# Attention and two MoE layers in one program: VectorE's small scratch tiles start one float32 column further in, and five one-column steps with two tensors take a column as scalar instead

## The chip, the cores and the metric

One Trainium2 chip, one core. The metric is the device time of one execution in microseconds (us); lower is better. A TensorE (PE), a VectorE (DVE), a ScalarE (ACT) and a GpSimd engine (POOL) work side by side, each through its own instructions in their order; SyncE (SP) issues the transfers.

## The reference

Chunked attention with 8 memory keys, then two feed-forward layers on the 3072 tokens that come out of it. What is computed, cut down:

```python
# q, k, v: (4, 8, 768, 64) float32; weights 512x2048 and 2048x512 (float64 words in memory)
for c in range(nc):                       # chunks of 32 queries, 16 left, 8 right
    k_full = concatenate([mem_k, k_ctx]); v_full = concatenate([mem_v, v_ctx])
    scores = scale * q_c @ k_full.T
    scores = scores - max(scores)
    a = exp(scores); a = a / (sum(a) + 1e-9)
    out[chunk] = a @ v_full
h = x @ w_in                              # first layer
g = maximum(h, 0) + alpha * minimum(h, 0)
x = g @ w_out
h = x @ w_in2                             # second layer
g = h * sigmoid(1.702 * h)
out = g @ w_out2
```

## The kernel before, in words

The tokens are cut into 12 blocks of 256. Products on TensorE are made from float16 parts, so every float32 operand is scaled by a power of two and split into a high part (ACT, L129, "hi") and a low part (VectorE, L132, "lo": the value times its scale less the high part).

The weights lie in memory as float64 words. `w_dec_b` (L200, L201, L207) makes float32 of them on VectorE with bit operations on 128x1024, with the sign for some by POOL (L205); `w_split_a` and `w_split_b` split them on ACT (L211) and POOL (L216). Their scales are worked out by `w_scale` (L179 to L189) on one or two columns.

Attention goes block by block: `att_scale` takes the maxima of q, k and v (three columns of `ar`) through `pow2_scale` (L108 to L112), L340 forms the scale of the exponential, then q, k and v are split (L129, L132). The scores of a block are made in two halves `i` by 16 matmuls each (L482, L483), copied from PSUM by ACT (`att_ext`, L497 and L499), and `att_smax` (L509, L510), `att_exp` (L514), `att_sum` (L519 to L523) and `att_a16` (L528, L529) follow. The block's output is scaled like q, through the same `pow2_scale` with one column (`att_xall`, L413, `att_xs`), and split to `xt`, on which layer 1 works.

Layer 1 is `h` on TensorE (L580), `t` on ACT (L615), `gf` on VectorE (L618), a split of `gf` to `g` (ACT L129 or L641 and L642; VectorE L132 or POOL L643) and the second matmul (L660). Layer 2 takes its operands in seven sums and differences (L591, L674), with `y_scale` (L715, L718) and `l2_scale` (L724 to `l2t`) ahead of each pair of blocks.

A table written by hand gives each function of attention, weights and evacuation a time; the order of the instructions on each engine is then set by the framework's scheduler from its own estimate of each instruction's duration (the `TileContext` is made with the timeline scheduling on). So an instruction of another kind can move others.

POOL works on 128x512 and 128x1024 tiles between VectorE's steps: L205, L216, L241, L510, L523, L529 and L643.

Of the kernel before, what the change touches and what calls it, by code (L numbers as in the profile page):

```python
# [8 lines left out]
F32 = mybir.dt.float32  # L9
# [4 lines left out]
ALU = mybir.AluOpType  # L14
# [22 lines left out]
def kernel(  # L37
# [14 lines left out]
    nc = tc.nc  # L52
    B, H, S, D = q.shape
# [16 lines left out]
    scale = 1.0 / float(D) ** 0.5  # L70

    HF = NP // 2
    const = ctx.enter_context(tc.tile_pool(name="const", bufs=1))
    sm_p = ctx.enter_context(tc.tile_pool(name="sm", bufs=2))
# [20 lines left out]
    wcs, winv, wful = ([const.tile([128, NP], F32, name=f"{n}{m}") for m in range(3)] for n in ("wcs", "winv", "wful"))  # L95
    for x in (wcs, winv, wful):
        x[2:] = [x[2][:, 0:HF], x[2][:, HF:NP]]
    l2t = const.tile([128, 2, HF], F32, name="l2t")
    l2t = [l2t[:, i] for i in range(2)]
    eye = const.tile([128, 128], F32, name="eye")  # L100
    make_identity(nc, eye)
    blk = [const.tile([128, 16], F32, name=f"blk{b}") for b in range(NB)]

    def pow2_scale(m, s, inv, lo):
        n = m.shape[1]
        t = sm_p.tile([128, 4], F32, tag="pt", name="pt", bufs=1)[:, 0:n]
        f = sm_p.tile([128, 4], F32, tag="pf", name="pf", bufs=1)[:, 0:n]
        nc.vector.tensor_scalar(out=t, in0=m, scalar1=lo, scalar2=None, op0=ALU.max)  # L108
        nc.vector.tensor_scalar(out=f.bitcast(U32), in0=t.bitcast(U32), scalar1=EXPM, scalar2=None, op0=ALU.bitwise_and)
        nc.vector.tensor_scalar(out=inv, in0=f, scalar1=2.0 ** -13, scalar2=None, op0=ALU.mult)  # L110
        nc.vector.reciprocal(out=t, in_=inv)
        nc.vector.tensor_scalar(out=s.bitcast(U32), in0=t.bitcast(U32), scalar1=EXPM, scalar2=None, op0=ALU.bitwise_and)  # L112
# [12 lines left out]
    def absmax(o, i):  # L125
        nc.vector.tensor_reduce(out=o, in_=i, axis=AX.X, op=ALU.max, apply_absolute_value=True)  # L126
# [46 lines left out]
    def w_scale(m, a, z):  # L173
        r = wmax[1][:, a:z] if m == 1 else wtmp.pop(("r", m, a))
        n = z - a
        ws = sm_p.tile([128, 6, 4], F32, tag="ws", name="ws")
        t, f, u, v, c, d = (ws[:, i, 0:n] for i in range(6))
        cs, inv, ful = wcs[m][:, a:z], winv[m][:, a:z], wful[m][:, a:z]
        nc.vector.tensor_scalar(out=t, in0=r, scalar1=2.0 ** -14, scalar2=1.0 / (1.375 if m > 1 else 1.625), op0=ALU.max, op1=ALU.mult)  # L179
        nc.vector.tensor_scalar(out=c, in0=r, scalar1=2.0 ** -14, scalar2=2.0 ** -112, op0=ALU.max, op1=ALU.mult)  # L180
        nc.vector.tensor_scalar(out=f.bitcast(U32), in0=t.bitcast(U32), scalar1=EXPM, scalar2=None, op0=ALU.bitwise_and)
        nc.vector.tensor_scalar(out=d.bitcast(U32), in0=c.bitcast(U32), scalar1=3, scalar2=EXPM, op0=ALU.logical_shift_left, op1=ALU.bitwise_and)
        nc.vector.reciprocal(out=v, in_=f)
        nc.vector.tensor_scalar(out=u, in0=f, scalar1=2.0 ** -113, scalar2=None, op0=ALU.mult)
        nc.vector.tensor_scalar(out=v, in0=v, scalar1=2.0 ** -111, scalar2=None, op0=ALU.mult)
        nc.vector.tensor_scalar(out=ful, in0=d, scalar1=2.0 ** -13, scalar2=None, op0=ALU.mult)
        nc.vector.tensor_scalar(out=cs.bitcast(U32), in0=v.bitcast(U32), scalar1=EXPM, scalar2=None, op0=ALU.bitwise_and)
        nc.vector.tensor_scalar(out=u.bitcast(U32), in0=u.bitcast(U32), scalar1=3, scalar2=None, op0=ALU.logical_shift_left)
        nc.vector.tensor_scalar(out=inv, in0=u, scalar1=2.0 ** 7, scalar2=None, op0=ALU.mult)  # L189
# [88 lines left out]
    att = {}  # L278

    def geo(nb):  # L280
        b, j = divmod(nb, S // TB)
        return b, j * TB

    def eng(nb):
        return nc.vector if nb == 0 else nc.gpsimd

    def bs(nb, i):
        return blk[nb][:, i:i + 1]
# [44 lines left out]
    def att_all(nb, a, z):  # L333
        att["r", nb] = all_max(blk[nb][:, a:z])

    def att_scale(nb, a, z):
        w = blk[nb]
        pow2_scale(att.pop(("r", nb)), w[:, 3 + a:3 + z], w[:, 6 + a:6 + z], 2.0 ** -30)
        if a == 0:
            nc.vector.scalar_tensor_tensor(out=w[:, 9:10], in0=w[:, 6:7], scalar=scale, in1=w[:, 7:8], op0=ALU.mult, op1=ALU.mult)  # L340

    def att_hi(nb, i):
        if i == 0:
# [66 lines left out]
        absmax(bs(nb, i), att["xp", nb, i].rearrange("p j t -> p (j t)"))  # L410

    def att_xall(nb):
        nc.vector.tensor_tensor(out=bs(nb, 2), in0=bs(nb, 0), in1=bs(nb, 1), op=ALU.max)  # L413
        att_all(nb, 2, 3)

    def att_xs(nb):
        w = blk[nb]
        pow2_scale(att.pop(("r", nb)), w[:, 9:10], w[:, 6:7], 2.0 ** -16)
        nc.vector.tensor_scalar(out=w[:, 8:9], in0=w[:, 6:7], scalar1=1.0 / AS, scalar2=None, op0=ALU.mult)
# [65 lines left out]
    def att_ext(nb, i):  # L485
        sc = at_p.tile([128, 9, SL], F32, tag="sc", name="sc", bufs=2)
        b, t0 = geo(nb)
        t1 = t0 + 128 * i
        sv = sc.rearrange("p (a b) s -> p a b s", a=3)
        pv = sps[:, :, 0:3 * TW].rearrange("p a (b t) -> p a b t", b=3)  # L490
        mo = 0 if i == 0 else BAND
        bo = NM if i == 0 else 0
        parts = [(sv, pv)]
        if nb in F32B:
            parts = [(sc[:, 0:6].rearrange("p (b a) s -> p a b s", a=2), pv[:, 0:2]), (sc[:, 6:8], pv[:, 2, 0:2])]
        for d, x in parts:
            nc.scalar.copy(d[..., WIN:SL], x[..., mo:mo + NM])  # L497
            for c in range(4):
                nc.scalar.copy(d[32 * c:32 * c + 32, ..., 0:WIN], x[32 * c:32 * c + 32, ..., bo + CH * c:bo + CH * c + WIN])  # L499
        if t1 == 0:  # L500
            eng(nb).memset(sc[0:32, 0:H, 0:LEFT], NEG)
        if t1 + 128 == S:
            nc.gpsimd.memset(sc[96:128, 0:H, WIN - RIGHT:WIN], NEG)
        att["s", nb, i] = sc[:, 0:H]

    def att_smax(nb, i):
        sc = att["s", nb, i]
        mx = at_p.tile([128, H, 1], F32, tag="mx", name="mx", bufs=2)
        nc.vector.tensor_reduce(out=mx, in_=sc, axis=AX.X, op=ALU.max)  # L509
        eng(nb).tensor_tensor(out=sc, in0=sc, in1=mx.to_broadcast([128, H, SL]), op=ALU.subtract)  # L510

# [3 lines left out]

    def att_sum(nb, i):
        sc = att["s", nb, i]
        sm = at_p.tile([128, H, 1], F32, tag="smm", name="smm", bufs=2)
        nc.vector.tensor_reduce(out=sm, in_=sc, axis=AX.X, op=ALU.add)  # L519
        nc.vector.tensor_scalar(out=sm, in0=sm, scalar1=1e-9, scalar2=1.0 / AS, op0=ALU.add, op1=ALU.mult)  # L520
        rs = at_p.tile([128, H, 1], F32, tag="rs", name="rs", bufs=2)
        nc.vector.reciprocal(out=rs, in_=sm)
        eng(nb).tensor_tensor(out=sc, in0=sc, in1=rs.to_broadcast([128, H, SL]), op=ALU.mult)  # L523

# [187 lines left out]

    def y_scale(sb):
        w, v = blk[2 * sb], blk[2 * sb + 1]
        nc.vector.tensor_tensor(out=w[:, 11:12], in0=w[:, 11:12], in1=v[:, 11:12], op=ALU.max)  # L715
        pow2_scale(w[:, 11:12], w[:, 12:13], w[:, 14:15], 2.0 ** -100)
        for x in (w, v):
            nc.vector.tensor_tensor(out=x[:, 10:11], in0=w[:, 12:13], in1=x[:, 8:9], op=ALU.mult)  # L718

    def l2_scale(sb):  # L720
        t = sm_p.tile([128, 1], F32, tag="l2", name="l2", bufs=1)
# [91 lines left out]
        nc.sync.dma_start(out=al, in_=alpha.rearrange("(f p) -> p f", p=128))  # L813

    def alpha_prep():
        t = sm_p.tile([128, 4], F32, tag="pt", name="pt", bufs=1)
        nc.vector.tensor_scalar(out=oma, in0=al, scalar1=-1.0, scalar2=1.0, op0=ALU.mult, op1=ALU.add)
        absmax(t[:, 0:1], al)
        amx = all_max(t[:, 0:1])
        nc.vector.tensor_scalar(out=t[:, 1:2], in0=amx, scalar1=1.0, scalar2=None, op0=ALU.max)  # L820
        nc.vector.tensor_scalar(out=t[:, 2:3].bitcast(U32), in0=t[:, 1:2].bitcast(U32), scalar1=EXPM, scalar2=None, op0=ALU.bitwise_and)
        nc.vector.tensor_scalar(out=kl[:, 1:2], in0=t[:, 2:3], scalar1=2.0 ** 23, scalar2=None, op0=ALU.mult)
        nc.vector.reciprocal(out=t[:, 3:4], in_=kl[:, 1:2])
        nc.vector.tensor_scalar(out=kl[:, 0:1].bitcast(U32), in0=t[:, 3:4].bitcast(U32), scalar1=EXPM, scalar2=None, op0=ALU.bitwise_and)
# [94 lines left out]
    for g in range(NP):  # L919
        m, p = 2 + g % 2, g // 2  # L920
        t = 24 * (g + 3) - 8 + EX3
# [12 lines left out]
    for b in range(NB):  # L934
        t = 3 * ((NP * (b + 1) if b >= NA else HF * (NA + b + 1)) + L0) + 2 - 3
# [7 lines left out]
    for sb in range(NB // 2):  # L943
        t = Q0 + 48 * sb
# [3 lines left out]
        t = 48 * sb + 80 if sb else 101.5  # L948
# [3 lines left out]
        if sb == NB // 2 - 1:  # L952
            t = Q0 + 20
# [11 lines left out]
    at_p = l1.enter_context(tc.tile_pool(name="at", bufs=1))  # L965
# [62 lines left out]
    for q in range(STEPS // 2 + LQ):  # L1028
        t = Q0 + 6 * q
# [13 lines left out]
        else:  # L1043
            while done < min(2 * STEPS // 2, 2 * q + 2 - LQ):
                u = units[done]
# [5 lines left out]
        if xs:  # L1051
            sb, p = divmod(q, NP)
# [33 lines left out]
```

## Time and profile before

| | |
|---|---|
| median of 3 runs | 1194.43 us (1193.17 to 1195.58) |
| span of the profiled execution | 1188.6 us |
| time of the profiled execution itself | not given apart from its span; the span lies 5.8 us below the median |
| TensorE matmul busy | 1079.9 us (91%) |
| VectorE busy | 854.5 us (72%), 1509 instructions |
| ScalarE busy | 633.0 us (53%) |
| GpSimd busy | 639.9 us (54%) |

The span is that of one execution, from its first instruction to its last; the busy shares are means over stages with different limits, so the stages are looked at one by one. A busy time contains what an instruction waits inside itself.

### The profile page before, as it was taken

What the parts mean: (1) busy time and instruction counts of PE and PEld (TensorE: products, weight loads), DVE (VectorE), ACT (ScalarE), POOL (GpSimd) and SP (SyncE); (2) the same over time, 40 slices, a digit from 0 to 9 for tenths busy, and PEclk for the clock granted to TensorE, in tenths of its full rate; (3) what the DMA queues carried; (4) which work ended last, traced back from release to release, by engine and by line L of the source; (5) the groups of instructions that cost most, each with busy time, mean ns of one, the idle gap of its engine ahead of it and who ended that gap; (6) DMA issues with size and microseconds to landing.
All of it is one profiled execution on the core that took longest, in us unless ns stands there. A gap on an engine that the chain in (4) does not pass through costs nothing.

```text
span 1188.6 us, 25661 instructions
## 1 busy us (share of the span) xinstructions
PE 1079.9 (91%) x10294; PEld 957.4 (81%) x10294; DVE 854.5 (72%) x1509; ACT 633.0 (53%) x968; POOL 639.9 (54%) x740
## 2 busy tenths in 40 slices
PE   4676788988989898999799999989999999999998
PEld 3665677977878787888698988878888888888887
DVE  6899995659778777858797634787676767667662
ACT  4567455556666476656665632545444444443442
POOL 1244542218666456617572811787685676666672
PEclk9668998999999899999899999999999999999999
DMA  9969328576999678888966380640110202000001
GB/s 203 308 126 194 90 72 172 83 145 180 228 219 257 136 203 172 229 151 197 191 184 139 108 345 19 266 170 19 58 41 6 76 19 80 20 6 14 19 19 37
DMA packets 250536, 154.53 MB, mean 130 GB/s; under 512 B 201200, under 2 KB 221680, under 8 KB 249392
## 3 DMA queue, kind: packets, MB, share of 16 engines
q1 hardware_dynamic: 250416, 152.88, 51.0%
q8 instruction: 81, 1.33, 0.5%
q14 instruction: 39, 0.32, 0.1%
HBM read 91.96 MB, written 38.93 MB: 110 GB/s over the span
## 4 chain that ended last, share of the span: by engine, by line
PE 50%; DVE 20%; DMA 11%; POOL 5%; issue 5%; ACT 5%; SPq 3%; ACTq 0%; POOLq 0%; DVEq 0%
PE acc L674 17%; PE x L591 16%; PE h L580 8%; PE acc L660 7%; DVE g L132 3%; DVE gf L618 2%; DMA q<-q 2%; POOL ga L625 2%; DVE wmax L126 2%; DMA wbig<-in_moe_w_in_dram 2%; DVE wr L200 1%; DMA kf<-in_k_dram 1%; DMA qf<-in_q_dram 1%; DMA w<-in_moe_w_in_dram 1%; DVE wr L201 1%
## 5 line engine op out<-in xcount | busy, mean ns | idle before, releaser
L625 POOL TENSOR_TENSOR ga<-ga 128x128 f32<-128x128 f32 x384 | 213.2, 580 | 172.2 <-DVE ga L623 160.1
L580 PE MATMUL h<-xt,wbig 128*128 128x256 f16 x2304 | 280.7, 280 | 21.0 <-ACT xt L129 15.0
L660 PE MATMUL acc<-g,wbig 128*128 128x256 f16 x2304 | 279.9, 279 | 13.1 <-DVE gf L618 6.2
L580 PEld LDWEIGHTS <-wbig 128*128 128x128 f16 x2304 | 230.9, 100 | 53.9 <-issue 22.6
L660 PEld LDWEIGHTS <-wbig 128*128 128x128 f16 x2304 | 229.3, 100 | 44.3 <-DVE gf L618 7.3
L674 PE MATMUL acc<-w2o,g 128*128 128x256 f16 x2016 | 231.6, 274 | 4.2 <-ACT g L129 3.4
L591 PE MATMUL x<-yt,w2i 128*128 128x256 f16 x2016 | 229.9, 273 | 0.9 <-DVE ha L601 0.9
L674 PEld LDWEIGHTS <-g 128*128 128x128 f16 x2016 | 197.4, 98 | 29.1 <-ACT g L129 4.4
L591 PEld LDWEIGHTS <-w2i 128*128 128x128 f16 x2016 | 197.4, 98 | 24.1 <-issue 1.1
L132 DVE SCALAR_TENSOR_TENSOR g<-ga,gk,g 128x896 f16<-128x896 f32 x96 | 121.1, 1267 | 91.0 <-ACT g L129 90.7
L129 ACT ACTIVATE g<-ga,gk 128x896 f16<-128x896 f32 x96 | 98.9, 1037 | 96.0 <-POOL ga L625 87.1
L618 DVE SCALAR_TENSOR_TENSOR gf<-t,oma,h 128x256 f32<-128x256 f32 x192 | 83.4, 472 | 75.0 <-ACT t L615 74.9
L615 ACT ACTIVATE t<-h 128x512 f32<-128x512 f32 x96 | 56.7, 591 | 66.8 <-PE h L580 38.8
L132 DVE SCALAR_TENSOR_TENSOR g<-gf,gk,g 128x512 f16<-128x512 f32 x81 | 77.8, 960 | 17.0 <-ACT g L129 16.7
L808 POOL TENSOR_TENSOR o<-o 128x256 f32<-128x256 f32 x77 | 74.4, 980 | 10.0 <-ACT o L803 9.5
L622 ACT ACTIVATE ga<-ha,l2t 128x512 f32<-128x512 f32 x48 | 34.4, 718 | 80.7 <-DVE ha L603 80.7
L230 POOL TENSOR_TENSOR wt<-wr 128x512 f32<-128x512 f32 x16 | 24.0, 1500 | 81.2 <-DVE wr L207 59.0
L216 POOL TENSOR_TENSOR wbig<-wr,wbig 128x1024 f16<-128x1024 f32 x16 | 35.5, 2229 | 53.4 <-ACT wbig L211 53.4
L129 ACT ACTIVATE g<-gf,gk 128x512 f16<-128x512 f32 x81 | 57.7, 712 | 0.5 <-DVE gf L618 0.4
L499 ACT COPY sc<-sps 32x504 f32<-32x504 f32 (+2 forms) x112 | 56.3, 502 | 1.0
L623 DVE SCALAR_TENSOR_TENSOR ga<-ga,ha 128x512 f32<-128x512 f32 x48 | 35.6, 742 | 21.0 <-ACT ga L622 21.0
L548 PEld LDWEIGHTS <-vbd 128*128 128x128 f16 x960 | 27.2, 99 | 28.7 <-issue 18.4
(194 smaller groups left out, 1521.9 us busy)
## 6 DMA issues: line engine op xcount, KB each, us to landing
yt_dr<-yh SPq DMA_DIRECT2D x42, 256.0 KB
yt<-yt_dr SPq DMA_DIRECT2D x42, 256.0 KB
w<-in_moe_w_in_dram SPq DMA_DIRECT2D x10, 1024.0 KB
w<-in_moe_w_out_dram SPq DMA_DIRECT2D x10, 1024.0 KB
vbd<-v_dr SPq DMA_DIRECT2D x80, 112.0 KB
w2i_dr<-wh SPq DMA_DIRECT2D x28, 256.0 KB
w2o_dr<-wh SPq DMA_DIRECT2D x28, 256.0 KB
w2i<-w2i_dr SPq DMA_DIRECT2D x4, 1792.0 KB
```

The source lines that it names most:

```text
L129: return nc.scalar.activation(out=hi, in_=src, func=ACTF.Copy, scale=s)
L132: return nc.vector.scalar_tensor_tensor(out=lo, in0=src, scalar=s, in1=hi, op0=ALU.mult, op1=ALU.subtract)
L499: nc.scalar.copy(d[32 * c:32 * c + 32, ..., 0:WIN], x[32 * c:32 * c + 32, ..., bo + CH * c:bo + CH * c + WIN])
L580: nc.tensor.matmul(out=hp[:, e], lhsT=w[:, wt, o:o + 128], rhs=x[:, xh, kk], start=(n == 0), stop=(n == 3 * KT - 1))
L591: nc.tensor.matmul(out=xs[bank][:, i], lhsT=w[:, o, wt, kk * 256 + c:kk * 256 + c + 128], rhs=yt[sb, yi][:, yh, kk], start=(n == 0), stop= ...
L615: nc.scalar.activation(out=t, in_=hp, func=ACTF.Relu, scale=-1.0)
L618: nc.vector.scalar_tensor_tensor(out=g[:, e], in0=t[:, e], scalar=oma[:, f:f + 1], in1=hp[:, e], op0=ALU.mult, op1=ALU.add)
L623: nc.vector.scalar_tensor_tensor(out=t, in0=t, scalar=1.0, in1=hp, op0=ALU.add, op1=ALU.mult)
L625: nc.gpsimd.tensor_tensor(out=g[:, out_], in0=g[:, x], in1=g[:, y], op=op)
L660: nc.tensor.matmul(out=acc[layer, b][dt // 2][:, dt % 2 * TB:(dt % 2 + 1) * TB], lhsT=w[:, wt, dt * 128:(dt + 1) * 128], rhs=g16[:, gh, e] ...
L674: nc.tensor.matmul(out=acc[layer, b][bank][:, i * 256:(i + 1) * 256], lhsT=g16[:, gh, gs], rhs=w[:, o, wt, p % 2], start=(p == 0 and n == ...
L808: e.tensor_tensor(out=ov[:, out_], in0=ov[:, x], in1=ov[:, y], op=op)
```

## The change

Two things are changed in the source.

The small scratch tiles of VectorE get spare columns, and what works on them starts at an odd column instead of column 0: `l2t`, `pt` and `pf` of `pow2_scale`, and the six rows of `ws` in `w_scale`. The tiles `mx`, `smm` and `rs` of `att_smax` and `att_sum` are no more; their eight columns now lie in the unused ninth row of the score tile `sc`, at its columns 1, 9 and 17.

Five one-column steps with two tensors (L340, L413, L715 and L718 in a loop of two) become `tensor_scalar`, with the second column handed over as the scalar. The number of VectorE instructions is 1509 as before. Behind L505 all lines stand 4 further down (L509 is L513 after, L615 is L619).

```diff
@@ -95,16 +95,16 @@
     wcs, winv, wful = ([const.tile([128, NP], F32, name=f"{n}{m}") for m in range(3)] for n in ("wcs", "winv", "wful"))
     for x in (wcs, winv, wful):
         x[2:] = [x[2][:, 0:HF], x[2][:, HF:NP]]
-    l2t = const.tile([128, 2, HF], F32, name="l2t")
-    l2t = [l2t[:, i] for i in range(2)]
+    l2t = const.tile([128, 2, HF + 2], F32, name="l2t")
+    l2t = [l2t[:, i, 1:HF + 1] for i in range(2)]
     eye = const.tile([128, 128], F32, name="eye")
     make_identity(nc, eye)
     blk = [const.tile([128, 16], F32, name=f"blk{b}") for b in range(NB)]
 
     def pow2_scale(m, s, inv, lo):
         n = m.shape[1]
-        t = sm_p.tile([128, 4], F32, tag="pt", name="pt", bufs=1)[:, 0:n]
-        f = sm_p.tile([128, 4], F32, tag="pf", name="pf", bufs=1)[:, 0:n]
+        t = sm_p.tile([128, 6], F32, tag="pt", name="pt", bufs=1)[:, 1:n + 1]
+        f = sm_p.tile([128, 6], F32, tag="pf", name="pf", bufs=1)[:, 1:n + 1]
         nc.vector.tensor_scalar(out=t, in0=m, scalar1=lo, scalar2=None, op0=ALU.max)
         nc.vector.tensor_scalar(out=f.bitcast(U32), in0=t.bitcast(U32), scalar1=EXPM, scalar2=None, op0=ALU.bitwise_and)
         nc.vector.tensor_scalar(out=inv, in0=f, scalar1=2.0 ** -13, scalar2=None, op0=ALU.mult)
@@ -173,8 +173,8 @@
     def w_scale(m, a, z):
         r = wmax[1][:, a:z] if m == 1 else wtmp.pop(("r", m, a))
         n = z - a
-        ws = sm_p.tile([128, 6, 4], F32, tag="ws", name="ws")
-        t, f, u, v, c, d = (ws[:, i, 0:n] for i in range(6))
+        ws = sm_p.tile([128, 6, 6], F32, tag="ws", name="ws")
+        t, f, u, v, c, d = (ws[:, i, 1:n + 1] for i in range(6))
         cs, inv, ful = wcs[m][:, a:z], winv[m][:, a:z], wful[m][:, a:z]
         nc.vector.tensor_scalar(out=t, in0=r, scalar1=2.0 ** -14, scalar2=1.0 / (1.375 if m > 1 else 1.625), op0=ALU.max, op1=ALU.mult)
         nc.vector.tensor_scalar(out=c, in0=r, scalar1=2.0 ** -14, scalar2=2.0 ** -112, op0=ALU.max, op1=ALU.mult)
@@ -337,7 +337,7 @@
         w = blk[nb]
         pow2_scale(att.pop(("r", nb)), w[:, 3 + a:3 + z], w[:, 6 + a:6 + z], 2.0 ** -30)
         if a == 0:
-            nc.vector.scalar_tensor_tensor(out=w[:, 9:10], in0=w[:, 6:7], scalar=scale, in1=w[:, 7:8], op0=ALU.mult, op1=ALU.mult)
+            nc.vector.tensor_scalar(out=w[:, 9:10], in0=w[:, 6:7], scalar1=scale, scalar2=w[:, 7:8], op0=ALU.mult, op1=ALU.mult)
 
     def att_hi(nb, i):
         if i == 0:
@@ -410,7 +410,7 @@
         absmax(bs(nb, i), att["xp", nb, i].rearrange("p j t -> p (j t)"))
 
     def att_xall(nb):
-        nc.vector.tensor_tensor(out=bs(nb, 2), in0=bs(nb, 0), in1=bs(nb, 1), op=ALU.max)
+        nc.vector.tensor_scalar(out=bs(nb, 2), in0=bs(nb, 0), scalar1=bs(nb, 1), scalar2=None, op0=ALU.max)
         att_all(nb, 2, 3)
 
     def att_xs(nb):
@@ -502,10 +502,14 @@
         if t1 + 128 == S:
             nc.gpsimd.memset(sc[96:128, 0:H, WIN - RIGHT:WIN], NEG)
         att["s", nb, i] = sc[:, 0:H]
+        att["sx", nb, i] = sc[:, H]
+
+    def spare(nb, i, a):
+        return att["sx", nb, i][:, a + 1:a + H + 1].rearrange("p (h t) -> p h t", t=1)
 
     def att_smax(nb, i):
         sc = att["s", nb, i]
-        mx = at_p.tile([128, H, 1], F32, tag="mx", name="mx", bufs=2)
+        mx = spare(nb, i, 0)
         nc.vector.tensor_reduce(out=mx, in_=sc, axis=AX.X, op=ALU.max)
         eng(nb).tensor_tensor(out=sc, in0=sc, in1=mx.to_broadcast([128, H, SL]), op=ALU.subtract)
 
@@ -515,10 +519,10 @@
 
     def att_sum(nb, i):
         sc = att["s", nb, i]
-        sm = at_p.tile([128, H, 1], F32, tag="smm", name="smm", bufs=2)
+        sm = spare(nb, i, H)
         nc.vector.tensor_reduce(out=sm, in_=sc, axis=AX.X, op=ALU.add)
         nc.vector.tensor_scalar(out=sm, in0=sm, scalar1=1e-9, scalar2=1.0 / AS, op0=ALU.add, op1=ALU.mult)
-        rs = at_p.tile([128, H, 1], F32, tag="rs", name="rs", bufs=2)
+        rs = spare(nb, i, 2 * H)
         nc.vector.reciprocal(out=rs, in_=sm)
         eng(nb).tensor_tensor(out=sc, in0=sc, in1=rs.to_broadcast([128, H, SL]), op=ALU.mult)
 
@@ -712,10 +716,10 @@
 
     def y_scale(sb):
         w, v = blk[2 * sb], blk[2 * sb + 1]
-        nc.vector.tensor_tensor(out=w[:, 11:12], in0=w[:, 11:12], in1=v[:, 11:12], op=ALU.max)
+        nc.vector.tensor_scalar(out=w[:, 11:12], in0=w[:, 11:12], scalar1=v[:, 11:12], scalar2=None, op0=ALU.max)
         pow2_scale(w[:, 11:12], w[:, 12:13], w[:, 14:15], 2.0 ** -100)
         for x in (w, v):
-            nc.vector.tensor_tensor(out=x[:, 10:11], in0=w[:, 12:13], in1=x[:, 8:9], op=ALU.mult)
+            nc.vector.tensor_scalar(out=x[:, 10:11], in0=w[:, 12:13], scalar1=x[:, 8:9], scalar2=None, op0=ALU.mult)
 
     def l2_scale(sb):
         t = sm_p.tile([128, 1], F32, tag="l2", name="l2", bufs=1)
@@ -813,7 +817,7 @@
         nc.sync.dma_start(out=al, in_=alpha.rearrange("(f p) -> p f", p=128))
 
     def alpha_prep():
-        t = sm_p.tile([128, 4], F32, tag="pt", name="pt", bufs=1)
+        t = sm_p.tile([128, 6], F32, tag="pt", name="pt", bufs=1)
         nc.vector.tensor_scalar(out=oma, in0=al, scalar1=-1.0, scalar2=1.0, op0=ALU.mult, op1=ALU.add)
         absmax(t[:, 0:1], al)
         amx = all_max(t[:, 0:1])
```

The scheduler sets other orders, chiefly for instructions that run from 78 to 150 us; further on few instructions move.

ACT, around 100 to 110 us. `sc<-sps` are the copies of block 2's scores, `xt<-xp` the high part of block 1's output, `junk` the maxima of block 3's k and q. Before:

```order
L204 ACTIVATE sgn<-w_485 128x1024
L129 ACTIVATE xt<-xp,blk_133 128x4x128 x2
L615 ACTIVATE t<-h 128x512
L211 CAST wbig<-wr 128x1024
L331 ACTIVATE junk,blk_135<-kf 128x1536
L497 COPY sc<-sps 128x9x8
L499 COPY sc<-sps 32x9x56 x4
L331 ACTIVATE junk,blk_135<-qf 128x1024
```

After:

```order
L211 CAST wbig<-wr 128x1024
L619 ACTIVATE t<-h 128x512
L497 COPY sc<-sps 128x9x8
L499 COPY sc<-sps 32x9x56 x4
L129 ACTIVATE xt<-xp,blk_133 128x4x128 x2
L331 ACTIVATE junk,blk_135<-kf 128x1536
L518 ACTIVATE sc<-sc,blk_134 128x512
```

The five copies of the first half of the scores have moved ahead of `xt` and of `junk<-kf`. On TensorE the 32 score matmuls of block 2 (L482, L483) now stand together; before, the second 16 stood behind 53 matmuls of `h`.

VectorE, at the same place: `v` is the low part of block 2's v, L108 to L112 with `pt` and `pf` the scales of block 1's output `blk_133`, L200 to L207 weights, `xt` the low part of block 1's output, `sc<-sc` after (L513) the score maximum that was `mx` before. Before:

```order
L132 SCALAR_TENSOR_TENSOR v_834<-vf,blk_134,v_834 128x1536
L122 TENSOR_REDUCE ar<-mx 128x1
L108 TENSOR_SCALAR pt<-ar 128x1
L109 TENSOR_SCALAR pf<-pt 128x1
L110 TENSOR_SCALAR blk_133<-pf 128x1
L200 TENSOR_SCALAR wr<-wr 128x1024
L111 RECIPROCAL pt<-blk_133 128x1
L419 TENSOR_SCALAR blk_133<-blk_133 128x1
L201 SCALAR_TENSOR_TENSOR wr<-wbig,wr 128x1024
L112 TENSOR_SCALAR blk_133<-pt 128x1
L207 SCALAR_TENSOR_TENSOR wr<-wbig,wr 128x1024
L132 SCALAR_TENSOR_TENSOR xt<-xp,blk_133,xt 128x4x128
```

After:

```order
L201 SCALAR_TENSOR_TENSOR wr<-wbig,wr 128x1024
L109 TENSOR_SCALAR pf<-pt 128x1
L207 SCALAR_TENSOR_TENSOR wr<-wbig,wr 128x1024
L110 TENSOR_SCALAR blk_133<-pf 128x1
L132 SCALAR_TENSOR_TENSOR v_822<-vf,blk_134,v_822 128x1536
L111 RECIPROCAL pt<-blk_133 128x1
L419 TENSOR_SCALAR blk_133<-blk_133 128x1
L126 TENSOR_REDUCE wmax_113<-wbig 128x1
L112 TENSOR_SCALAR blk_133<-pt 128x1
L622 SCALAR_TENSOR_TENSOR gf<-t,oma,h 128x256 x2
L513 TENSOR_REDUCE sc<-sc 128x8
L132 SCALAR_TENSOR_TENSOR xt<-xp,blk_133,xt 128x4x128 x2
```

The v step has moved behind the weight steps, between L110 and L111; `xt` has moved behind a maximum, `gf` and the score maximum.

ACT, around 146 to 151 us: `wbig<-wr` is the cast of decoded weights, `t` the activation's part of `h`. Before:

```order
L699 COPY yf<-acc 128x512 x2
L211 CAST wbig<-wr 128x1024 x2
L615 ACTIVATE t<-h 128x512
L129 ACTIVATE g_1522<-gf,gka 128x512
L194 ACTIVATE wr<-wbig,wcs_118 128x1024
```

After:

```order
L703 COPY yf<-acc 128x512 x2
L211 CAST wbig<-wr 128x1024
L619 ACTIVATE t<-h 128x512
L211 CAST wbig<-wr 128x1024
L129 ACTIVATE g_1504<-gf,gka 128x512
```

`t` now stands between the two casts instead of behind both.

## Rows read from the trace of the kernel before

**Rows 1.** The page, its first line:

```profile
span 1188.6 us, 25661 instructions
```

**Rows 2.** Stretches: length; busy PE, PEld, DVE, ACT, POOL (instructions); granted clock; DMA share, GB/s.

```profile
93.00:193.00 100.00, 81.63 (x773) 70.71 (x774) 91.57 (x158) 58.12 (x82) 44.64 (x25) 0.94 0.50 117
...
262.00:724.00 462.00, 424.81 (x4431) 377.50 (x4430) 339.16 (x603) 280.14 (x443) 255.84 (x204) 0.97 0.77 191
724.00:1189.00 465.00, 454.27 (x4137) 404.75 (x4134) 313.44 (x513) 208.55 (x300) 300.00 (x472) 0.99 0.16 55
```

**Rows 3.** VectorE's groups, shapes apart: busy us, mean ns | idle before.

```profile
L109 DVE TENSOR_SCALAR pf<-pt 128x3 uint32<-128x3 uint32 x10 | 9.7, 972 | 0.0
...
L340 DVE SCALAR_TENSOR_TENSOR blk<-blk 128x1 f32<-128x1 f32 x10 | 4.9, 494 | 0.0
...
L711 DVE TENSOR_SCALAR blk<-ar,blk 128x1 f32<-128x1 f32 x12 | 2.5, 208 | 0.2
...
L112 DVE TENSOR_SCALAR blk<-pt 128x3 uint32<-128x3 uint32 x10 | 1.6, 162 | 0.0
...
L109 DVE TENSOR_SCALAR pf<-pt 128x1 uint32<-128x1 uint32 x8 | 1.2, 149 | 0.2
```

**Rows 4.** Chain of waits, 93 to 193 us: start us, us, what.

```profile
115.84 0.95 DVE ws L180
...
117.93 0.78 DVE wcs L187
...
123.88 1.04 DVE ws L188
...
165.31 1.48 DVE ws L179
...
178.29 2.02 DVE pt L108
...
180.38 2.02 DVE pf L109
```

**Rows 5.** Timeline: start us, us, engine, line; in brackets idle time ahead, releaser.

```profile
118.62 0.15 DVE L189 TENSOR_SCALAR winv<-ws 128x2 f32<-128x2 f32 x1
118.64 1.16 POOL L643 TENSOR_TENSOR g<-gf,g 128x512 f16<-128x512 f32 x1
...
177.12 5.25 POOL L216 TENSOR_TENSOR wbig<-wr,wbig 128x1024 f16<-128x1024 f32 x2 [10.35 <-ACT wbig L211]
...
184.84 1.82 DVE L132 SCALAR_TENSOR_TENSOR k<-kf,blk,k 128x1536 f16<-128x1536 f32 x1 [0.87 <-ACT k L129]
...
338.83 2.27 POOL L241 TENSOR_TENSOR wh<-wt,wh 128x512 f16<-128x512 f32 x2 [1.32 <-ACT wh L240]
...
339.06 0.94 DVE L340 SCALAR_TENSOR_TENSOR blk<-blk 128x1 f32<-128x1 f32 x1
...
339.93 0.15 DVE L112 TENSOR_SCALAR blk<-pt 128x3 uint32<-128x3 uint32 x1
```

**Rows 6.** Chain of waits, 262 to 724 us: first and last of thirteen pieces.

```profile
283.89 1.05 DVE pf L109
...
617.55 1.05 DVE pf L109
```

**Rows 7.** Timeline around the gaps of VectorE, 104 to 151 us.

```profile
105.41 4.64 PE L580 MATMUL h<-xt,wbig 128*128 128x256 f16 x41 [0.88 <-DVE xt L132]
...
105.89 2.31 ACT L499 COPY sc<-sps 32x504 f32<-32x504 f32 x4
...
108.23 0.69 DVE L509 TENSOR_REDUCE mx<-sc 128x8 f32<-128x512 f32 x1 [2.10 <-ACT sc L499]
...
113.90 0.69 DVE L509 TENSOR_REDUCE mx<-sc 128x8 f32<-128x512 f32 x1 [0.74 <-POOL sc L503]
...
148.64 1.04 ACT L211 CAST wbig<-wr 128x1024 f16<-128x1024 f32 x1 [1.52 <-POOL wr L205]
...
150.22 0.87 DVE L618 SCALAR_TENSOR_TENSOR gf<-t,oma,h 128x256 f32<-128x256 f32 x2 [4.23 <-ACT t L615]
```

## The prediction

> **What bounds the kernel now.** The busy times by stretch were read first [rows 2]. From 93 to 193 us VectorE works 91.57 of 100 us and no other engine comes near that: it decodes weights, computes the activation and prepares attention all at once. From 262 to 724 us TensorE works 424.81 of 462 us, from 724 us on 454.27 of 465: there a VectorE or GpSimd step counts only where TensorE happens to wait for it, and behind 724 us hardly at all. So the change is priced in 93 to 193 us, at part value in 262 to 724 us, and at nothing behind.
>
> Next came VectorE's groups with shapes kept apart [rows 3]. The same mask line L109 lasts 972 ns on 128x3 and 149 ns on 128x1. Three numbers a row instead of one can't cost 0.8 us. Then the chain of waits [rows 4] and the timeline [rows 5]: small operations that look long end when a GpSimd operation ends. L108 and L109 took 2.10 and 2.05 us on the chain at 178.29 and 180.38, under two GpSimd products L216 that ran from 177.12 for 5.25 us in all. L340 began at 339.06 and ended at 340.00; the first of the two products at L241, half of 2.27 us from 338.83, ends at about 339.97. So some VectorE instructions can't run beside a GpSimd instruction. One-source operations on two or more columns wait so, one-column ones with an immediate don't (149 ns), and L340, one column but two tensors, does: 494 ns mean of ten.
>
> [...]
>
> **The change, part by part.** No instruction is added or taken away; three things can move the time.
>
> *(a) The odd column.* pt, pf, ws, l2t and the columns of mx, smm and rs now start at an odd column. By itself this moves 4 bytes and costs nothing. It gains if an operation that starts at an odd column no longer waits for GpSimd. What that would be worth comes from the pieces of the chain.
> In 93 to 193 us six of them are such waits: 0.95 (L180), 0.78 (L187), 1.04 (L188), 1.48 (L179), 2.02 (L108), 2.02 (L109), sum 8.29 [rows 4]. Freed they cost 0.15 each at most, as L189 at 118.62 does [rows 5]. L180, L187 and L179 give 3.21 − 0.45 = 2.8. L188's is given back, since the next step, the big L200, is such an operation itself and would wait for the same GpSimd product. Of the 4.04 of L108 and L109 not all is left: the k lo step (L132, two SBUF inputs) starts at 184.84 [rows 5], and would have to wait for L216 to end at 177.12 + 5.25 = 182.37; 184.84 − 182.37 is 2.4 (estimate). Together 5.2 us.
> In 262 to 724 us the chain has thirteen such pieces, L340's not among them, from L109 at 283.89 to L109 at 617.55 [rows 6], 12.6 us, or 10.6 without the 0.15 that each takes when free. TensorE is idle there for 37 of 462 us, and a freed step is late only until the next transfer or matmul; I take half, 5.3.
> So (a) lies between 0 and 10.5 us (18.0 if nothing were given back: 8.29 − 0.9 + 10.6). No row of before shows an odd-column operation alone under GpSimd. The nearest is L112, which writes columns 3 to 5 on three columns: 162 ns mean of ten [rows 3], never blocked. But where GpSimd worked beside it, it came right behind a step that had just been released, as at 339.93 behind L340 [rows 5], and an operation on even columns got through in the same way: L189, 0.15 at 118.62, while GpSimd's L643 is shown from 118.64. This row is no evidence for the offset. What the rows do tie the wait to is the number of columns, 972 against 149, and the offset changes no number of columns. I take 0.
>
> [...] No run here shows an odd start by itself.
>
> *(b) The one-column steps.* L340 (ten instructions [rows 3]), L413 (two), L715 (six) and L718 (twelve), 30 in all, become one-source steps with a pointer to a column. The rows' price of that form is L711: 208 ns, never blocked [rows 3], against 149 free. So an unblocked one loses 0.06, 1.8 us for all thirty if all lay on the path, some 0.4 for those ahead of 262 us. A blocked L340 gains 0.7 in itself. But right behind L340 stands L112 on 128x3, one source: if width decides, L112 now waits for the end of the same GpSimd product, and ACT's k step, which waits for L112, starts no earlier. I take 0 gain, 0.4 loss.
>
> *(c) The order.* With the kinds of instructions changed, the scheduler sets other orders from 78 to 150 us. Three gaps of VectorE lie there [rows 7]: 2.10 before 108.23 (for the four score copies of block 2, L499, 2.31 us on ACT from 105.89, with ACT's xt and junk ahead of them), 0.74 before 113.90 (for the second half of the scores, whose 16 products stand behind 41 matmuls of h from 105.41, 4.64 us), and 4.23 before 150.22 (for t, which stands behind the cast L211 at 148.64, that waited 1.52 for GpSimd). After, the copies stand ahead of xt and junk, the score products stand together ahead of the h matmuls, and t stands between the two casts. The first two gaps can go whole, 2.84. Of the third only about 0.6 can: L618 can start early, but the g step behind it needs ACT's g, which is still behind the second cast, to 148.64 + 1.04. So −3.4 if all of it comes, 0 if the gaps only change places; I take −3.4, since VectorE is the bound there and has other work ready.
>
> Sum: (a) 0, (b) +0.4, (c) −3.4: −3.0 us. The profiled execution spans 1188.6 us [rows 1] and the median of the runs is 1194.43, 5.8 more; I take the difference as it is and work from the median: 1194.43 − 3.0 = **1191.4 us**. About 0.2%, 2.4 us, is what a measurement of this kernel can tell from no change: faster begins below 1192.0, slower above 1196.8.
>
> **The rivals.**
> *The offset frees them.* For it: the waits are real, and L112 was never caught. Against: each of its passes has another reason. Then −3.0 − 5.2 − 5.3 = −13.5; a gain in the middle of a kernel whose last 465 us are TensorE's carries less than whole, at 0.8 it is −11: 1183, between 1181 (the 13.5 whole) and 1190 (only part of the first stretch), and down to 1173 by the bound of 18.0 with (c) whole. [...]
> *The new order stalls* (slower). In the new order VectorE's L112 of block 1 stands behind the v step and a maximum, ACT's xt behind the five copies, and VectorE's xt behind L618 and the score maximum. Before, the h matmuls of block 1 waited for that xt until 105.41 [rows 7]. What is put in its way now is 2.31 on ACT and 0.87 + 0.69 on VectorE, 3.9 at most, and if the scores are late, all of it. VectorE then lacks h to work on; it loses what it can't fill, none of (c)'s gain comes, and (b) costs 0.4 to 1.8: +3 to +5, about 1198. It decides from where the h matmuls that start at 105.41 start later than 108. Against it: VectorE has weight decoding ready to fill, and the scores' operands are there early.
> *Nothing of it shows*: gaps change places, (b) costs 0.4: 1194.8. This is the upper edge of my own case.
>
> **How the numbers follow.** My case 0.50 (1187 to 1196: (c) whole and some of L340's gain down to nothing), the offset 0.34 (1173 to 1190), the stall 0.16 (1195 to 1200). Faster: 0.50 × 0.55 + 0.34 × 0.96 = 0.60. Same: 0.50 × 0.32 + 0.34 × 0.03 + 0.16 × 0.25 = 0.21. Slower: the rest, 0.19. The range 1178 to 1198 leaves out the best tail of the second case and the worst half of the third, under 2 in 10.
>
> **What would show it.** (a): L109 on 128x3 still near 1 us in the mean, L180, L187, L108 still ending with GpSimd operations, is right; 0.15 to 0.2 everywhere is wrong, and then the time is near 1183. (b): L340 at 0.2 in all ten, and L112 in its place up to 0.9. (c): the gap before the second block's score maximum gone, and VectorE's busy share in 93 to 193 us above 0.92 with the stretch 3 us shorter. Wrong altogether I am if matmuls of h start later than 108 and VectorE idles more there than before.

## The result and the profile after

The changed kernel takes 1182.67 us (median of 4, 1181.47 to 1183.31) beside 1193.8 us of the kernel before on the same chip: ratio 0.9909, interval 0.9895 to 0.9923. Run again in a later group it took 1181.04 us, ratio 0.9907 (0.9887 to 0.9927). That is 11 us, 0.9%, where 3 us were forecast; the time lies inside the range, near the rival "the offset frees them" (1183). The experiments show that it came there by another road, so that the range holding it is luck.

The page of the changed kernel, beside [rows 1]; line numbers behind L505 are 4 higher from here on:

```profile
span 1180.6 us, 25668 instructions
...
PE 1076.3 (91%) x10294; PEld 954.4 (81%) x10294; DVE 851.2 (72%) x1509; ACT 631.9 (54%) x968; POOL 641.4 (54%) x740
```

Its stretches, columns as in [rows 2]:

```profile
93.00:193.00 100.00, 84.97 (x805) 74.13 (x804) 87.97 (x159) 62.24 (x86) 44.29 (x26) 0.94 0.52 129
...
262.00:724.00 462.00, 426.02 (x4444) 378.62 (x4443) 338.69 (x603) 274.93 (x434) 254.11 (x202) 0.97 0.73 189
724.00:1189.00 465.00, 444.99 (x4064) 396.87 (x4061) 308.16 (x503) 206.46 (x296) 299.23 (x472) 1.00 0.16 54
```

From 93 to 193 us TensorE does more (84.97 for 81.63 us) and VectorE is busy for less (87.97 for 91.57). Counting the same matmuls of h (L580 before, L584 after) in both traces, the later kernel is 3.2 us ahead at 138 us, 9.0 at 220, 7.3 at 305 and 8.0 at 700, and nothing is won behind. The profiled execution after took 1182.36 us, 1.8 more than its span. The same 1.8 stands between time and span in every later run; with it the profiled execution of before took about 1190.4, which is below the four of its group (1192.9 to 1195.58) and within the later ones (1187.86 to 1196.58). This is why the traces differ by 8.0 and the medians by 11.

VectorE's groups after, which answer to [rows 3] (busy us, mean ns):

```profile
L109 DVE TENSOR_SCALAR pf<-pt 128x3 uint32<-128x3 uint32 x10 | 7.7, 772 | 0.0
...
L112 DVE TENSOR_SCALAR blk<-pt 128x3 uint32<-128x3 uint32 x10 | 4.5, 452 | 0.0
...
L340 DVE TENSOR_SCALAR blk<-blk 128x1 f32<-128x1 f32 x10 | 1.8, 184 | 0.0
...
L109 DVE TENSOR_SCALAR pf<-pt 128x1 uint32<-128x1 uint32 x8 | 1.2, 149 | 0.1
```

And two places of its timeline (start us, us, engine, line):

```profile
122.43 2.58 POOL L216 TENSOR_TENSOR wbig<-wr,wbig 128x1024 f16<-128x1024 f32 x1
...
122.94 2.09 DVE L179 TENSOR_SCALAR ws<-ar 128x2 f32<-128x2 f32 x1
124.95 0.16 DVE L180 TENSOR_SCALAR ws<-ar 128x2 f32<-128x2 f32 x1
...
332.71 1.27 POOL L230 TENSOR_TENSOR wt<-wt,wr 128x512 f32<-128x512 f32 x1
332.79 0.18 DVE L340 TENSOR_SCALAR blk<-blk 128x1 f32<-128x1 f32 x1
332.90 1.10 DVE L112 TENSOR_SCALAR blk<-pt 128x3 uint32<-128x3 uint32 x1
```

The odd column frees nothing. L112, which now reads column 1 of pt and writes column 3 of blk, starts at 332.90 inside GpSimd's L230 (to 333.98) and ends at 334.00; L179, writing column 1 of ws, starts inside L216 (to 125.01) and ends at 125.03. Of the 143 TENSOR_SCALAR operations on two to eight columns 42 last over 0.25 us after, 41 before. In either trace 39 of them start 0.02 us or more behind a GpSimd TENSOR_TENSOR that has 0.3 us or more to go, and all 39 last over 0.25 us. L340 itself no longer waits, 184 ns instead of 494, and L112 behind it waits in its place: 452 instead of 162.

### The profile page after: what moved, and what is told of

It is laid out like the page before. It is cut to its first block, busy times and chain, and to the rows that moved or that the text cites. A ratio compares the mean times of both kernels' runs of the same rounds, so it can differ in the third digit from the quotient of the medians.

```text
span 1180.6 us, 25668 instructions
## 1 busy us (share of the span) xinstructions
PE 1076.3 (91%) x10294; PEld 954.4 (81%) x10294; DVE 851.2 (72%) x1509; ACT 631.9 (54%) x968; POOL 641.4 (54%) x740
## 4 chain that ended last, share of the span: by engine, by line
PE 46%; DVE 20%; DMA 12%; POOL 7%; ACT 6%; issue 5%; SPq 3%; ACTq 0%; POOLq 0%; DVEq 0%
PE acc L678 17%; PE x L595 16%; PE acc L664 6%; PE h L584 6%; DVE g L132 3%; DMA qf<-in_q_dram 3%; DVE gf L622 3%; DMA w<-in_moe_w_in_dram 2%; POOL ga L629 2%; DMA q<-q 2%; DVE wr L200 2%; DMA wbig<-in_moe_w_in_dram 1%; DVE wr L201 1%; DVE wmax L126 1%; DVE wr L207 1%
## 5 line engine op out<-in xcount | busy, mean ns | idle before, releaser
L584 PE MATMUL h<-xt,wbig 128*128 128x256 f16 x2304 | 279.6, 279 | 14.2 <-ACT xt L129 11.7
L584 PEld LDWEIGHTS <-wbig 128*128 128x128 f16 x2304 | 230.4, 100 | 46.5 <-issue 15.6
L132 DVE SCALAR_TENSOR_TENSOR g<-gf,gk,g 128x512 f16<-128x512 f32 x81 | 82.3, 1016 | 16.3 <-ACT g L129 16.2
L619 ACT ACTIVATE t<-h 128x512 f32<-128x512 f32 x96 | 56.8, 591 | 62.4 <-PE h L584 33.3
L230 POOL TENSOR_TENSOR wt<-wr 128x512 f32<-128x512 f32 x16 | 24.0, 1498 | 78.4 <-DVE wr L207 74.5
L216 POOL TENSOR_TENSOR wbig<-wr,wbig 128x1024 f16<-128x1024 f32 x16 | 37.1, 2321 | 49.3 <-ACT wbig L211 49.3
L241 POOL TENSOR_TENSOR wh<-wt,wh 128x512 f16<-128x512 f32 x32 | 44.6, 1402 | 11.4 <-ACT wh L240 11.4
```

Source lines behind the costliest of these rows:

```text
L132: return nc.vector.scalar_tensor_tensor(out=lo, in0=src, scalar=s, in1=hi, op0=ALU.mult, op1=ALU.subtract)
L241: nc.gpsimd.tensor_tensor(out=hv[:, 1], in0=src, in1=hv[:, 0], op=ALU.subtract)
L584: nc.tensor.matmul(out=hp[:, e], lhsT=w[:, wt, o:o + 128], rhs=x[:, xh, kk], start=(n == 0), stop=(n == 3 * KT - 1))
L619: nc.scalar.activation(out=t, in_=hp, func=ACTF.Relu, scale=-1.0)
```

## The experiments

Three groups of four, each kernel beside the kernel before on its chip (median 1192.39, 1192.44 and 1192.68 us).

**Is it the odd column, L340 or the rest?** Theories: the order that L340's new kind brings makes the gain; the odd columns make it; L340's own wait makes it. All tiles back to even columns:

```diff
-    l2t = [l2t[:, i, 1:HF + 1] for i in range(2)]
+    l2t = [l2t[:, i, 0:HF] for i in range(2)]
...
-        return att["sx", nb, i][:, a + 1:a + H + 1].rearrange("p (h t) -> p h t", t=1)
+        return att["sx", nb, i][:, a:a + H].rearrange("p (h t) -> p h t", t=1)
```

> The changed kernel with every small tile back on even start columns (0 in pt, pf, ws, l2t; 0, 8 and 16 for mx, smm, rs), one-tensor steps kept; the order on every engine is that of the changed kernel. If the odd column is worth nothing and the new order or L340 makes the gain: within 1.5 us of the changed kernel, about 1183, ratio to before 0.990 to 0.992, and the two- and three-column operations wait for GpSimd as they do there. If the odd column makes most of it: 1188 to 1193.

1184.3 us, ratio 0.9938 (0.9925 to 0.9951): most of the gain stays. It is within the expected 1.5 us of 1183, but its ratio missed 0.990 to 0.992.

The tile edits of the change alone, on odd columns, without the five one-tensor steps:

> The kernel before with the odd columns alone (no step made one-tensor); the order on every engine is that of before. If the odd column is worth nothing: 1192.5 to 1195.5, the same as before, and L108, L109, L180, L187 still end with GpSimd operations. If it makes the gain: 1183 to 1188 and these operations at 0.15.

1186.65 us, ratio 0.996 (0.9946 to 0.9973). Neither theory had this: the time falls by 4.8 us by the ratio (5.7 between the medians), but the waits are all there, 42 of the 143 over 0.25 us:

```profile
L109 DVE TENSOR_SCALAR pf<-pt 128x3 uint32<-128x3 uint32 x10 | 10.4, 1042 | 0.0
```

L340 alone:

```diff
-            nc.vector.scalar_tensor_tensor(out=w[:, 9:10], in0=w[:, 6:7], scalar=scale, in1=w[:, 7:8], op0=ALU.mult, op1=ALU.mult)
+            nc.vector.tensor_scalar(out=w[:, 9:10], in0=w[:, 6:7], scalar1=scale, scalar2=w[:, 7:8], op0=ALU.mult, op1=ALU.mult)
```

> The kernel before with L340 alone made one-tensor (ten instructions); this gives the changed kernel's order from 78 to 150 us, but not its small moves after 300 us. If L340, by its kind or by the order that it brings, makes the gain: 1182 to 1186. If L413, L715 and L718 or their order are needed: 1188 to 1194.

1186.19 us, ratio 0.9951 (0.9939 to 0.9962), just above the first range: L340 alone brings 5.8 us by the ratio (6.2 between the medians).

The change without L340's edit (the line above the other way round in the changed kernel):

> The changed kernel with L340 alone put back to two tensors: the order of before up to 300 us, small moves after. If L340 makes the gain: 1191 to 1195. If the steps L413, L715 and L718 or the moves after 300 us make it: 1183 to 1188.

1189.25 us, ratio 0.9975 (0.9966 to 0.9985), between the two expectations. So there are two causes of about equal size: one hangs on L340, one on the tiles, and the tiles' one isn't a wait that went away. This run differs from the one with the tile edits alone by L413, L715 and L718 and is 2.6 us slower in the medians; the intervals overlap, and no run has these twenty steps by themselves.

**L340: its wait or the order?** The order on every engine was held by ordering edges without any wait. The order of the L340 run, put on the kernel before (ORDER lists, engine by engine, the instructions that stood elsewhere):

```diff
+    at = {x.name: x for x in nc.cur_bb.bb.instructions}
+    dep = mybir.DependencyInfo(mybir.DependencyClass.NoSync, mybir.DependencyReason.DATA)
+    for row in ORDER:
+        for u, w in zip(row, row[1:]):
+            tc.add_manual_dep(at[f"I-{w}"], f"I-{u}", dep, reason="order")
```

> The kernel before, L340 left with two tensors, but the instructions of all engines put in the order that they have when L340 is one-tensor. If the order makes L340's gain: 1185 to 1188 as with L340 changed. If L340's own wait makes it: 1191 to 1194.

1186.93 us, ratio 0.9954 (0.9938 to 0.9971). And the one-tensor L340 in the order of before:

> The kernel before with L340 one-tensor, but all engines held in the order of before. If the order makes L340's gain: 1191 to 1194. If L340's own wait makes it: 1185 to 1188; L112 behind it waits in L340's place if a one-source step on three columns can't run beside GpSimd.

1191.55 us, ratio 0.9995 (0.9984 to 1.0007). The order makes all of it; the edit itself is worth nothing that can be measured, and L112 waits in L340's place:

```profile
L112 DVE TENSOR_SCALAR blk<-pt 128x3 uint32<-128x3 uint32 x10 | 4.8, 479 | 0.0
...
L340 DVE TENSOR_SCALAR blk<-blk 128x1 f32<-128x1 f32 x10 | 1.8, 183 | 0.0
```

What the order changed is seen in VectorE's groups from 78 to 144 us. Before:

```profile
L200 DVE TENSOR_SCALAR wr<-wr 128x1024 uint32<-128x1024 uint32 x6 | 9.4, 1559 | 0.0
...
L132 DVE SCALAR_TENSOR_TENSOR g<-gf,gka,g 128x512 f16<-128x512 f32 x4 | 6.6, 1679 | 0.0
L132 DVE SCALAR_TENSOR_TENSOR v<-vf,blk,v 128x1536 f16<-128x1536 f32 x1 | 3.8, 3833 | 0.0
...
L132 DVE SCALAR_TENSOR_TENSOR k<-kf,blk,k 128x1536 f16<-128x1536 f32 x1 | 3.3, 3291 | 0.0
...
L132 DVE SCALAR_TENSOR_TENSOR q<-qf,blk,q 128x1024 f16<-128x1024 f32 x1 | 2.3, 2336 | 0.0
```

With the order alone:

```profile
L200 DVE TENSOR_SCALAR wr<-wr 128x1024 uint32<-128x1024 uint32 x7 | 5.9, 837 | 0.6 <-ACT wr L194 0.6
L132 DVE SCALAR_TENSOR_TENSOR g<-gf,gka,g 128x512 f16<-128x512 f32 x4 | 4.8, 1208 | 0.0
...
L132 DVE SCALAR_TENSOR_TENSOR v<-vf,blk,v 128x1536 f16<-128x1536 f32 x1 | 2.0, 1953 | 0.0
...
L132 DVE SCALAR_TENSOR_TENSOR k<-kf,blk,k 128x1536 f16<-128x1536 f32 x1 | 1.8, 1806 | 0.0
...
L132 DVE SCALAR_TENSOR_TENSOR q<-qf,blk,q 128x1024 f16<-128x1024 f32 x1 | 1.3, 1271 | 0.0
```

The same instructions are shorter: v 1953 ns for 3833, k 1806 for 3291, q 1271 for 2336, L200 837 for 1559 in the mean (seven of them for six). Before, q, k, v and four of the six L200 (1523 to 2572 ns) start inside a GpSimd TENSOR_TENSOR; the two L200 that start outside take 680 and 681, and of the four g two inside take 2616 and 2619, two outside 740 and 742. In the new order six of the seven L200 take 0.64 to 0.69 us and three of the four g 0.74 or 0.75. v shows it. Before, it starts just behind GpSimd's L205, which ends at 95.42:

```profile
93.29 2.13 POOL L205 TENSOR_TENSOR wr<-wr,sgn 128x1024 f32<-128x1024 f32 x1 [1.23 <-DMA q<-q]
...
93.33 3.83 DVE L132 SCALAR_TENSOR_TENSOR v<-vf,blk,v 128x1536 f16<-128x1536 f32 x1
```

With the order alone it starts ahead of the next GpSimd operation:

```profile
97.72 1.95 DVE L132 SCALAR_TENSOR_TENSOR v<-vf,blk,v 128x1536 f16<-128x1536 f32 x1
...
98.65 2.98 POOL L216 TENSOR_TENSOR wbig<-wr,wbig 128x1024 f16<-128x1024 f32 x1 [4.34 <-ACT wbig L211]
```

Over VectorE's instructions 151 to 252, which are the same set in both orders, the busy time falls from 63.2 to 58.8 us; the stretch gets only 2.7 us shorter (66.2 to 63.5), since its idle time grows by 1.7: VectorE, now early, waits for transfers too. With the 1.1 us by which the set starts earlier (k lies ahead of it) it ends 3.8 us earlier. VectorE's waits in this run from 85 to 185 us (us in total, times, longest):

```profile
DVE gf L618 <- ACT t L615: 1.7, 1, 1.7
...
DVE wmax L126 <- DMA wbig<-in_moe_w_out_dram: 1.5, 1, 1.5
...
DVE blk L126 <- DMA vf<-in_mem_v_dram: 0.8, 1, 0.8
```

**The tiles: odd columns, moved tiles, or where all the rest lies?** The spare columns make small tiles larger, and tiles are laid out one behind the other: the first ones behind l2t lie 32 bytes further on, and the larger ones behind ws lie 160 bytes further on. Among these are kf, qf, vf and vbd, into which attention's transfers write pieces of 256 bytes; they start at 0 modulo 64 bytes instead of 32. The tiles that stood behind mx, smm and rs lie 32 bytes lower, and xt, wbig and what follows wbig stay. First l2t as it was, in the changed kernel:

```diff
-    l2t = const.tile([128, 2, HF + 2], F32, name="l2t")
-    l2t = [l2t[:, i, 1:HF + 1] for i in range(2)]
+    l2t = const.tile([128, 2, HF], F32, name="l2t")
+    l2t = [l2t[:, i] for i in range(2)]
```

> The changed kernel with l2t alone as before (no spare columns, start column 0); the order on every engine stays. l2t's 16 bytes less make every tile behind it lie 32 bytes lower, so that kf, qf, vf and vbd start at 32 modulo 64 bytes as in the kernel before, instead of 0. If the part of the gain that the tiles brought comes from where the transfers' destinations lie: 1185 to 1188, and the mean of a 256-byte packet goes from 22.7 ns back to above 24, the share of the transfer queue to above 50%. If it comes from the odd columns, or from the move of mx, smm and rs: 1181.5 to 1183.5.

In its group stood the changed kernel itself:

> The changed kernel itself, to have it beside the others of this group: 1181.5 to 1183.5, ratio to before 0.990 to 0.992.

The narrow l2t took 1183.2 us, ratio 0.9919 (0.9897 to 0.9940), beside 1181.04, 0.9907, of the changed kernel: 2 us slower in the medians, the intervals overlap, inconclusive. The expectation of the transfer theory, 1185 to 1188 and packets above 24 ns, did not come: the time is in the other theory's range and the queue's share was 49.6%. But this edit takes back only 32 of the 160 bytes.

Then the same question with the order of before, so that only the layout differs. The wide tiles on even columns:

> The kernel before (all steps and their order as there) with the tiles of the changed kernel, wide and with mx, smm and rs in the score tile, but on even columns. Everything behind l2t lies 32 bytes further on, kf, qf, vf and vbd 160. If where the tiles lie, or the move of mx, smm and rs, made what the odd columns seemed to bring (1186.65 against 1192.39): 1186 to 1189, ratio 0.995 to 0.997, and a 256-byte packet takes 23.4 ns or less. If the odd columns made it: 1191 to 1194.

1188.03 us, ratio 0.9964 (0.9950 to 0.9977): as on odd columns (0.9960). mx, smm and rs moved, kf, qf, vf and vbd where they lay (the tiles that stood behind mx, smm and rs lie 192 bytes lower):

```diff
-        mx = at_p.tile([128, H, 1], F32, tag="mx", name="mx", bufs=2)
+        mx = spare(nb, i, 0)
```

> The kernel before with mx, smm and rs alone moved into the ninth row of the score tile, on even columns; kf, qf, vf and vbd stay where they lie in before (32 modulo 64 bytes). If where the transfers' destinations lie makes the gain: 1191 to 1194, a 256-byte packet at 24 ns or more. If the move of the three tiles makes it: 1186 to 1189.

1191.58 us, ratio 1.0002 (0.9988 to 1.0015): nothing. And this kernel with l2t two columns wider and used as before, which does nothing but push the tiles behind it, up to xt, 32 bytes on:

```diff
-    l2t = const.tile([128, 2, HF], F32, name="l2t")
-    l2t = [l2t[:, i] for i in range(2)]
+    l2t = const.tile([128, 2, HF + 2], F32, name="l2t")
+    l2t = [l2t[:, i, 0:HF] for i in range(2)]
```

> The run with mx, smm and rs moved, and l2t two columns wider but used from column 0: everything behind it lies 32 bytes further on, kf, qf, vf and vbd at 0 modulo 64 bytes. If the 64 bytes decide: 1186 to 1189, a 256-byte packet at 23.4 ns or less. If it takes the larger shift of the changed kernel: as the run without the 32 bytes.

1187.4 us, ratio 0.9958 (0.9942 to 0.9973). Thirty-two bytes of empty space bring 4 us. Both kernels have the same instructions in the same order on every engine, and VectorE, ScalarE and GpSimd are busy for nearly the same time (857.9 and 856.3, 631.7 and 632.1, 639.8 and 639.2 us). TensorE's busy time falls from 1081.8 to 1077.2, but the kernel before, as slow as the one without the bytes, had 1079.9. Counted by the matmuls of h, the bytes are 1.2 us ahead at 220 us and 3.7 at 700; the order alone was 4.4 ahead of the kernel before at 220 and 3.6 at 700. So the order gains early, and the layout later on. The transfers' queue (packets, MB, share of the 16 engines' span) without these bytes:

```profile
q1 hardware_dynamic: 250416, 152.88, 50.2%
```

with them:

```profile
q1 hardware_dynamic: 250416, 152.88, 49.4%
```

and in the changed kernel:

```profile
q1 hardware_dynamic: 250416, 152.88, 49.3%
```

The number of packets and bytes is the same; they take less time. The mean of the 188,928 packets of 256 bytes, worked out from the packet records of each trace: 24.1 to 24.8 ns in the five kernels with the layout of before (before, L340 alone, order alone, kind alone, moved tiles), 22.5 to 23.4 in those laid out further on. With l2t narrow, 128 bytes further on but again at 32 modulo 64, it is 23.3, so that the remainder modulo 64 is not the whole rule. Modulo 256 bytes the four tiles start at 32 before, at 64 with the 32 bytes alone, at 160 with l2t narrow and at 192 in the changed kernel. By the kernel's transfers 123,648 of these packets go to the four tiles; the others go from tile to tile (into kt, q1 and aT), and these tiles moved as well. Which tile and which remainder counts is not shown, nor is it shown wait by wait how shorter packets make the kernel shorter.

Last, the changed kernel with 32 bytes behind wbig, to push the long transfers' destinations as well:

> The changed kernel with 32 bytes of padding behind wbig, so that wbig (twelve 1 MB transfers of the first 100 us) and xt start at 0 modulo 64 bytes too. If the place of a transfer's destination costs time for long packets as well: 1179 to 1181.5. If it matters only for 256-byte packets, or not at all: 1181 to 1183.5, as the changed kernel.

1182.34 us, ratio 0.9920 (0.9905 to 0.9935): no gain. By its ratio no version beat the changed kernel.

## Why the prediction was right and wrong

**(a) The odd column** was taken at 0 for the waits, and that step held: L109, L179 and L112 wait on odd columns as on even ones (L109 772 ns in the mean after and 1042 with the tile edits alone, for 972 before; L179 2.09 and L112 1.10 us after). With the order of before odd and even columns take the same time (0.9960, 0.9964). With the changed order even columns were at 0.9938 and odd ones at 0.9909 and 0.9907; of these two intervals one ends just below that of the even columns and one overlaps it, and no run settles whether a difference is left there. The step that failed is "By itself this moves 4 bytes and costs nothing". It moves the tiles behind l2t, and that is worth 4 to 5 us: 1187.4 against 1191.58 for 32 bytes alone. The diff shows the wider tiles; I followed the columns and not the layout, and transfers were in no term, though their engines are busy for 0.77 of the time from 262 to 724 us [rows 2]; after, it is 0.73.

Two readings on the way were off. "One-source operations on two or more columns wait so" does not hold for RECIPROCAL: before, 11 such steps on two to eight columns start inside a GpSimd TENSOR_TENSOR, and none lasts over 0.25 us. And the 2.10 and 2.05 us of L108 and L109 are those of the timeline; the chain has 2.02 for each, with which the sum was made.

**(b) The one-column steps** were taken at a loss of 0.4 us. For L340 in the old order no gain was measured (0.9995, which can't tell 0.4 from 0), and for the reason given, since L112 takes over the wait (479 ns in the mean for 162). The other twenty were not run by themselves.

**(c) The order** had the right sign and was mis-sized: 5.5 us (1186.93 against 1192.44) where 3.4 were taken. The mechanism that I named, gaps that close, carries little of it. The gaps after, beside [rows 7]:

```profile
102.26 0.69 DVE L513 TENSOR_REDUCE sc<-sc 128x8 f32<-128x512 f32 x1 [1.44 <-ACT sc L499]
...
131.64 0.69 DVE L200 TENSOR_SCALAR wr<-wr 128x1024 uint32<-128x1024 uint32 x1 [0.59 <-ACT wr L194]
...
141.72 0.87 DVE L622 SCALAR_TENSOR_TENSOR gf<-t,oma,h 128x256 f32<-128x256 f32 x2 [1.74 <-ACT t L619]
143.99 0.90 DVE L132 SCALAR_TENSOR_TENSOR g<-gf,gka,g 128x512 f16<-128x512 f32 x1 [1.39 <-ACT g L129]
...
145.66 1.78 DVE L200 TENSOR_SCALAR wr<-wr 128x1024 uint32<-128x1024 uint32 x1 [0.76 <-ACT wr L194]
```

The gap of 0.74 is gone, 2.10 has become 1.44 and 4.23 has become 1.74 and 1.39, the second just where the step was expected to be held, by ACT's g: some 2.5 us in all, of which two new gaps (0.59 and 0.76, L200 for ACT's wr) take half back. All waits of VectorE from 85 to 185 us sum to 7.9 us before and 7.6 after. The gain came out of the instructions: 4.4 us of busy time with the order alone, waits behind GpSimd inside the big splits and shifts (v's 3833 ns for 1953 is one), which look like work. I had priced such waits only for the small operations. So the sign that I gave for (c), a busy share above 0.92, was the wrong way round: it fell to 0.88.

**The sum.** Order 0.9954 times layout 0.9960 gives 0.9914, the change but for 0.0005. The same product for the changed kernel on even columns is 0.9954 times 0.9964, or 0.9918; measured were 0.9938, and these 2.4 us no run explains. In the traces the two causes meet: with the order alone VectorE waits 1.5 and 0.8 us for wbig and vf; in the changed kernel's waits of the same stretch one line of transfers is left:

```profile
DVE wmax L126 <- DMA w<-in_moe_w_in_dram: 0.2, 1, 0.2
```

**The rivals.** "The offset frees them" hit the time, 1183, by a mechanism that no run showed. "The new order stalls" did not happen: h's matmuls of block 1 begin before 108, and VectorE had work:

```profile
104.36 1.96 PE L584 MATMUL h<-xt,wbig 128*128 128x256 f16 x12
...
106.61 1.58 PE L584 MATMUL h<-xt,wbig 128*128 128x256 f16 x13
```

The layout was no rival at all. The range held the time only because a rival with a wrong mechanism had the right price.

## What to carry to other kernels

A wider small tile moves the tiles behind it, here by 32 bytes for l2t's 16. Before pricing such an edit, list the start addresses before and after, above all of what many short transfers write to; and to test it, widen a tile without using the new columns. Where VectorE and GpSimd share work, a long VectorE instruction may be about half waiting: compare the same instruction's duration across the traces (v 3833 ns behind L205, 1953 with the order alone) before calling a busy engine a bound. And where a scheduler sets the order, hold the order fixed to tell what an edit does from what the reordering does.

## What the runs showed of the hardware that was not expected

256-byte packets took 24.1 to 24.8 ns in one layout and 22.5 to 23.4 in layouts 32, 128 or 160 bytes further on, with the same packets in the same number; 32 bytes of shift alone changed the kernel by 4 us. In every one of these runs most of these packets took 18 ns; what changes is how many took longer: 57 to 60% took 18 ns in the five kernels with the layout of before, 61 to 66% in all others. Longer packets did not gain: 96.7 ns before and 96.4 after for 2048 bytes. Why is open: the run with l2t narrow speaks against 0 modulo 64 bytes as the only rule.

Whether a VectorE step waited for GpSimd went by its kind and width: in the trace of before 39 of 39 TENSOR_SCALAR steps on two to eight columns that started inside a GpSimd TENSOR_TENSOR with 0.3 us or more to go lasted 372 ns or more, and none of 30 on one column (at most 216 ns) and none of 11 RECIPROCAL steps on two to eight columns (at most 203 ns) waited.
